# A second order for the same 2445 operations: a two-layer attention and token-MLP kernel whose schedule is a stored list

## The chip, the cores and the metric

The kernel runs on one core of one Trainium2 chip. The metric is the device time of one execution in microseconds (us). Three timed runs of the kernel before gave 452.30, 452.40 and 452.86 us, a median of 452.4 us. One further execution was recorded by the profiler.

## The reference

The input is one sequence of 2048 tokens with 512 features in bf16. Two kinds of block follow each other, each with a layer norm before it and a residual addition after it, and the pair is done twice with the same weights. In the text, layer 0 and layer 1 are the two repetitions.

```python
x = A_x
x = x + _A_ref(_layernorm(x), A_wqkv, A_wo)
x = x + _B_ref(_layernorm(x), B_w1, B_b1, B_w2, B_b2)
x = x + _A_ref(_layernorm(x), A_wqkv, A_wo)
x = x + _B_ref(_layernorm(x), B_w1, B_b1, B_w2, B_b2)
# _A_ref: 32 heads of 16 features; a token sees itself and the 255 before it
scores = einsum("bhqd,bhkd->bhqk", q, k) * 16 ** -0.5      # masked to the window, softmax
o = einsum("bhqk,bhkd->bhqd", softmax(scores), v);  return o @ wo
# _B_ref: an MLP over the tokens, 2048 -> 1792 -> 2048, after a second layer norm
u = gelu(einsum("bsd,sf->bdf", h, w1) + b1);  return einsum("bdf,fs->bds", u, w2) + b2
```

## The kernel before

**The operations.** The kernel first records 2445 operations in a graph (`Graph.op`, L117), each with what it reads and writes. A list then says in which order they are replayed, and for 199 of them which of two or three engines does the work. Line numbers are those of the kernel before; in the kernel after, everything below the list stands 10 lines higher.

On TensorE (915 operations, 6420 matmuls) there are five families.

- A *score* (`f_sc`, L694) multiplies queries and keys of one group of heads. Four heads run in the four row strips of the array at the same time. A score fills two pairs of PSUM banks. There are 76 scores in each layer.
- A *pv* (`f_pv`, L747) multiplies probabilities by values, with 64 by 32 tiles of the array. It needs the exponentials of several scores and their masks.
- *Projections*: queries and keys (`proj`, L566), values (`vproj`, L623, in 64-column tiles), and the output projection (`wo_block`, L783).
- *u*: the first product of the MLP. Most of it (`u_part`, L842) is done while attention still runs, for the token blocks that are ready; the last token blocks come in `u_last` (L861, matmuls at L868).
- *y*: the second product of the MLP (`y_block`, L887), 16 blocks of 7 operations in each layer. The y of layer 0 runs partly beside the attention of layer 1. The y of layer 1 ends the kernel.

All projections, u pieces and y pieces go through one helper, `mm_group`, so that their matmuls have one line, L519. (L521 is the same work done as two 64-column halves, which is used after a value projection.) An operation of `mm_group` is two matmuls of 512 columns.

Beside TensorE: ScalarE does two exponentials for each score (L709), one for each pair of banks, and the gelu (L883). GpSimd multiplies each probability tile with its masks (L730), and takes the power for the layer norm (L490). VectorE does the statistics and the normalising (L477, L479, L497), the transposed read of the attention output out of PSUM (*od*, L767), the reciprocal (L771), a second transpose (*od2*, L778), and the residual additions (L789, L895).

**Choices of engine.** These operations have an alternative: the copies out of PSUM (*evt* L562, *evq* L577, *evk* L599, *evv* L642, *evu* L853) run on VectorE or ScalarE; the first key tiles (*evka*, L588 or L587) run on VectorE or ScalarE; the spreading of keys with zeros (*kz*) is eight small DMAs on the SyncE queue (L608), or two multiplications on GpSimd or VectorE (L613); the product of the attention output with the reciprocal (*prod*, L773) runs on GpSimd or VectorE.

**What sets the order.** Nothing is scheduled when the kernel is built. `begin_order` (L54) unpacks a stored string, `ORDER`, into pairs of an operation and the number of its alternative:

```python
k, alt = divmod(lo + 256 * hi, 4)
out.append((left.pop(k), alt))
```

`Graph.replay` (L185) goes through that list, puts each operation at the end of its engine's program, and hands out buffers as it goes: eight PSUM banks, six probability tiles, four tiles for w1 and so on. A buffer goes to the operation that comes next in the list, and that operation then waits for the buffer's last users (`_take`, L164). So the list settles three things: the order on each engine, the engine, and which earlier work each buffer waits for. `Graph.emit` (L206) writes the programs and their waits. SyncE issues all DMAs in the order of the list, and a DMA that must wait holds up those behind it.

## Time and profile before

| what | value |
|---|---|
| timed runs | 452.30, 452.40, 452.86 us (median 452.4) |
| span of the profiled execution (first to last instruction) | 447.8 us |
| PE busy | 426.7 us (95%) |
| ACT busy | 316.8 us (71%) |
| DVE busy | 307.4 us (69%) |
| POOL busy | 232.2 us (52%) |
| DMA | 41.21 MB, 92 GB/s in the mean |

The profile gives the span of its execution, 447.8 us, and no time of its own beside it. The span is 4.6 us under the median of the timed runs, since these also hold what lies before the first and after the last instruction.

PE stands for TensorE, PEld for its weight loads, DVE for VectorE, ACT for ScalarE, POOL for GpSimd, and SPq for the queue of SyncE. A matmul counts as busy from its start to its modelled end (379 ns for 512 columns), although the next may start 216 ns after it. A PE that is busy throughout is therefore not always a full PE, and distances between starts tell more than busy time.

### The profile page before, as it was taken

The numbers are of one execution on the slowest core, as the hardware profiler recorded it, in microseconds if no ns is written. First come the engines' busy times: TensorE is split into PE (matmuls) and PEld (weight loads), VectorE is DVE, ScalarE is ACT, GpSimd is POOL, SyncE is SP. The second block draws the span as 40 slices with busy tenths as digits, with TensorE's granted clock in tenths as the row PEclk, the third lists the DMA queues.
The fourth block names the chain that finished last, engine by engine and source line by source line (L and its number), as shares of the span: only waits on it lengthen the run. The fifth ranks groups of instructions, "written<-read, shape, count | busy, mean of one in ns | idle before, by whom it ended". The sixth has DMA issues, their size and how long they took to land.

```text
span 447.8 us, 14720 instructions
## 1 busy us (share of the span) xinstructions
PE 426.7 (95%) x6420; PEld 200.4 (45%) x6420; DVE 307.4 (69%) x558; ACT 316.8 (71%) x362; POOL 232.2 (52%) x350
## 2 busy tenths in 40 slices
PE   7988997999989999999999999999899999999997
PEld 6644443334433444444644444444343444444443
DVE  7999789788895478555876767888765577430233
ACT  4999999999898931704898999999999880430000
POOL 5587989866776531010556687768775651000000
PEclk9999999999998999999999999999999999999999
DMA  8240604101153358522132240241223237654435
GB/s 240 68 120 16 132 3 107 15 7 22 25 150 91 73 161 228 144 58 70 26 38 72 57 95 20 55 115 42 51 52 88 74 107 212 174 154 119 119 94 189
DMA packets 95136, 41.21 MB, mean 92 GB/s; under 512 B 33632, under 2 KB 95072, under 8 KB 95072
## 3 DMA queue, kind: packets, MB, share of 16 engines
q1 hardware_dynamic: 95072, 40.27, 35.1%
q8 instruction: 51, 0.84, 0.8%
q14 instruction: 13, 0.11, 0.1%
HBM read 33.56 MB, written 2.10 MB: 80 GB/s over the span
## 4 chain that ended last, share of the span: by engine, by line
PE 65%; ACT 23%; POOL 5%; DVE 4%; DMA 2%; SPq 1%; issue 1%; POOLq 0%
PE PS L519 39%; ACT pt L709 23%; PE PS L868 7%; PE PS L694 7%; PE PS L747 6%; POOL pt L730 4%; PE PS L631 3%; PE PS L521 2%; SPq L608 1%; PE PS L399 1%; DMA w1b<-in_B_w_dram 1%; DVE xh_sb L497 1%; DMA kbd<-stg 1%; DVE rl L767 1%; DVE ul L773 1%
## 5 line engine op out<-in xcount | busy, mean ns | idle before, releaser
L709 ACT ACTIVATE pt<-PS 128x1024 bf16<-128x1024 f32 (+1 forms) x304 | 280.8, 1041 | 19.8 <-PE PS L694 19.2
L730 POOL TENSOR_TENSOR pt<-pt,ldm 128x256 int32<-128x256 int32 (+2 forms) x270 | 176.7, 679 | 74.7 <-ACT pt L709 73.9
L519 PE MATMUL PS<-xh_sb,w1b 128*128 128x512 bf16 x270 | 68.0, 386 | 1.8 <-DVE xh_sb L497 0.8
L694 PE MATMUL PS<-qT,kbd 32*128 32x256 bf16 (+4 forms) x1488 | 60.6, 252 | 6.9 <-ACT pt L709 4.3
L519 PE MATMUL PS<-uT,w2b 128*128 128x512 bf16 x268 | 66.2, 380 | 0.0
L519 PE MATMUL PS<-xhT,wqkv 128*128 128x512 bf16 (+1 forms) x254 | 58.6, 354 | 2.5 <-ACT pt L709 1.0
L490 POOL TENSOR_TENSOR rstd<-agg,mhalf 128x2 f32<-128x2 f32 (+1 forms) x33 | 22.6, 688 | 67.8 <-DVE agg L479 67.7
L767 DVE STREAM_TRANSPOSE rl<-PS 128x1024 f32<-128x1024 f32 x32 | 39.9, 1247 | 22.3 <-PE PS L747 22.0
L895 DVE SCALAR_TENSOR_TENSOR x_sb<-PS,b2col,x_sb 128x512 bf16<-128x512 f32 x32 | 23.6, 742 | 45.0 <-PE PS L519 44.9
L694 PEld LDWEIGHTS PS<-qT,kbd 32*128 32x128 bf16 x1488 | 21.9, 92 | 61.3 <-ACT pt L709 46.1
L883 ACT ACTIVATE uT<-rl,b1col 128x512 bf16<-128x512 f32 x28 | 18.7, 714 | 42.1 <-DVE rl L879 41.7
L747 PE MATMUL PS<-pt,vb 64*32 64x320 bf16 (+4 forms) x2976 | 44.9, 253 | 3.3 <-POOL pt L730 2.0
L477 DVE BATCH_NORM_STATS2 stats<-x_sb 128x6 f32<-128x512 bf16 x64 | 42.9, 678 | 1.4 <-DMA x_sb<-in_A_x_dram 0.7
L519 PE MATMUL PS<-uT,pt 128*128 128x512 bf16 x166 | 40.7, 379 | 0.0
L747 PEld LDWEIGHTS PS<-pt,vb 64*32 64x32 bf16 x2976 | 29.0, 89 | 22.1 <-POOL pt L730 12.6
L868 PE MATMUL PS<-xh_sb,w1b 128*128 128x512 bf16 x168 | 38.6, 379 | 0.2 <-DMA w1b<-in_B_w_dram 0.2
L519 PEld LDWEIGHTS PS<-xh_sb,w1b 128*128 128x128 bf16 x270 | 23.2, 99 | 34.6 <-issue 8.3
L519 PEld LDWEIGHTS PS<-uT,w2b 128*128 128x128 bf16 x268 | 24.5, 98 | 30.3 <-issue 3.2
L631 PE MATMUL PS<-wqkv,xhT 128*64 128x256 bf16 x512 | 35.9, 276 | 1.1 <-ACT pt L709 0.9
L519 PEld LDWEIGHTS PS<-xhT,wqkv 128*128 128x128 bf16 x254 | 21.2, 98 | 26.3 <-issue 4.3
L497 DVE TENSOR_SCALAR xh_sb<-x_sb,agg,rstd 128x512 bf16<-128x512 bf16 x64 | 29.3, 492 | 4.3 <-POOL rstd L490 4.1
L519 PE MATMUL PS<-wo_sb,oT 128*128 128x512 bf16 x122 | 30.6, 380 | 0.6 <-ACT pt L709 0.6
(66 smaller groups left out, 353.2 us busy)
## 6 DMA issues: line engine op xcount, KB each, us to landing
w1b<-in_B_w_dram SPq DMA_DIRECT2D x112, 128.0 KB, 2.8
w2b<-in_B_w_dram SPq DMA_DIRECT2D x70, 128.0 KB, 2.4
pt<-in_B_w_dram SPq DMA_DIRECT2D x42, 128.0 KB, 2.8
out_dram<-x_sb SPq DMA_DIRECT2D x16, 128.0 KB, 1.9
x_sb<-in_A_x_dram SPq DMA_DIRECT2D x3, 512.0 KB, 7.6
kbd<-stg SPq DMA_DIRECT2D x88, 16.0 KB, 1.9
wqkv<-in_A_wqkv_dram SPq DMA_DIRECT2D x4, 256.0 KB, 4.3
wqkv<-in_A_wqkv_dram SPq DMA_DIRECT2D x1, 512.0 KB, 7.0
```

Source lines behind the costliest of these rows:

```text
L477: op("vector:stat", lambda e: e.bn_stats(st[:, 0:6], x_sb[:, t, :]), reads=[f"x{t}"], writes=[("st", i)], cost=dve_cost(512), after=late_s ...
L490: op("gpsimd:rstd", lambda e: e.tensor_tensor(rstd[:, t0:t1, 0], agg[:, t0:t1, 1], mhalf[:, 0:1].to_broadcast([P, t1 - t0]), op=ALU.pow), ...
L497: op("vector:xh", lambda e: e.tensor_scalar(xh_sb[:, t, :], x_sb[:, t, :], agg[:, t, 0:1], rstd[:, t, :], op0=ALU.subtract, op1=ALU.mult), ...
L519: return e.matmul(o, lhsT=w, rhs=x, start=start, stop=stop, skip_group_check=True)
L631: last = e.matmul(bank(ft)[64 * j:64 * j + 64, sc * 256:(sc + 1) * 256], lhsT=xhT[:, tx.slot, c, tok:tok + 64], rhs=wqkv[:, c, 1024:1536]. ...
L694: last = e.matmul(bank(tt[r // 2], r % 2)[:, base + c0 * 64:base + (c0 + n) * 64], lhsT=kbd[32 * r:32 * r + 32, tk.slot, o, jj].rearrange( ...
L709: op("scalar:exp", lambda e, ts=ts, tp=tp, i=i, cols=cols: e.activation(probs(tp)[:, i, 0:cols, :], pair(ts)[:, :, 0:cols].rearrange("p r ...
L730: return e.tensor_tensor(v, v, m, op=ALU.mult)
L747: last = e.matmul(bank(t, h)[32 * r:32 * r + 32, i + q0 * 64:i + (q0 + n) * 64], lhsT=vb[64 * h:64 * h + 64, tk.slot, jj, 4 * o + r, :], r ...
L767: op("vector:od", lambda e, t=tod, tr=tr: e.transpose(rl[:, tr.slot:tr.slot + 2].rearrange("p a b -> p (a b)"), pair(t)), reads=[(tod, i) ...
L868: last = e.matmul(bank(tu, tt), lhsT=v()[:, sc - b0, k0 + tt * P:k0 + (tt + 1) * P], rhs=xh_sb[:, sc, :], start=(sc == b0), stop=(sc == NT ...
L895: op("vector:resy", lambda e: e.scalar_tensor_tensor(x_sb[:, t, :], bank(ft), b2col[:, t:t + 1], x_sb[:, t, :], op0=ALU.add, op1=ALU.add), ...
```

## The change

Only the stored list is replaced. The computation, the sizes, the buffers and the 2445 operations are the same.

```diff
@@ -13,42 +13,32 @@
 ORDER = (
-    'c-qZYJ&5bd6&~5MH}gP&d7!{tP(Z~zP(TC)ROo>o=z#(%6i}hUg$WL*P~pOb3Kb40;KBhHE*wzd!i5SKE?l^9z=aDJE?hX^!o?O2Y~f-',
...
-    'cI+e3L@e4F@kU-y*E#Om5eue-MHQ4AiU_zwVEIC*8S=4>(AaL2tSD4&-+(GKtH=K;SCD};TI|Ym$v@`qvAXq'
+    'c-qZYEvV~S7G7!hc`q~M!hVnkxsZWe$UsCy9%LXQ19^~v3`9h9AR-J$R8&MnRD>a-qM`#85fv2`6%}Eq=s+GsR8&+{R8&+{R8$;MQBiTk5f!u2)1JS3?'
...
+    '6v%IE{{b$XL=O'
 )
```

Unpacked, the two lists differ in the following.

- *Position.* 86 of the 2445 operations keep their place in the list.
- *Engine.* 48 of the 199 choices differ. The number of operations goes from 543 to 555 on VectorE, from 360 to 357 on ScalarE, from 338 to 333 on GpSimd and from 289 to 285 on SyncE (a kz on SyncE, eight DMAs, counted as one). TensorE keeps its 915.
- *prod* goes from 18 on GpSimd and 14 on VectorE to 15 and 17. *kz* goes from 11 on SyncE, 8 on GpSimd and 5 on VectorE to 7, 7 and 10.
- *TensorE.* The scores follow each other in the same sequence. What stands between two scores differs. The array changes between its four layouts (whole, 64-column halves, row strips, 64 by 32 tiles) 350 times, 346 before. Before the first score stand the same six operations.
- *Between the layers*, from the last score of layer 0 to the first of layer 1, stand 47 y operations, 52 before. The other five now stand between scores of layer 1.
- *SyncE.* The first ten loads are as before. The load of x for tokens 1536 to 2047 now stands ahead of the first four transposing DMAs; before, it stood behind them. Weight loads for w1 and w2 are spread differently throughout.
- *The start on ScalarE and VectorE.* The filling of one constant value tile moves from GpSimd to ScalarE, ahead of its first copy; of the first two key tiles one was spread on VectorE and one on ScalarE, and now ScalarE does both, while VectorE takes the first query copies.

## The prediction

> **What bounds the kernel now.** I read the page first: the shares of the engines, and the slices.

> ```profile
> span 447.8 us, 14720 instructions
> PE 426.7 (95%) x6420; PEld 200.4 (45%) x6420; DVE 307.4 (69%) x558; ACT 316.8 (71%) x362; POOL 232.2 (52%) x350
> PE   7988997999989999999999999999899999999997
> ACT  4999999999898931704898999999999880430000
> ```

> TensorE is nearly always busy, ScalarE only in two long stretches: the attention of either layer. So I cut the span at the first and last score of each layer and asked for the busy time in these five stretches (columns: stretch, its length, then each engine's busy time).

> ```profile
> 0.00:8.90 8.90, 5.93 (x56) 5.26 (x56) 5.61 (x17) 2.83 (x5) 5.41 (x15) 1.00 0.76 206
> 8.90:157.10 148.20, 136.02 (x2796) 65.18 (x2796) 120.71 (x226) 139.74 (x156) 110.96 (x162) 0.99 0.29 68
> 157.10:209.80 52.70, 52.68 (x355) 24.20 (x355) 35.43 (x66) 17.28 (x24) 6.81 (x11) 1.00 0.50 140
> 209.80:362.70 152.90, 150.02 (x2737) 68.60 (x2736) 113.18 (x199) 141.82 (x158) 103.80 (x155) 1.00 0.27 60
> 362.70:447.80 85.10, 82.02 (x479) 37.20 (x478) 32.51 (x53) 15.14 (x22) 5.26 (x9) 1.00 0.52 149
> ```

> In layer 0 (8.9 to 157.1) ScalarE is busy 139.7 of 148.2 us and TensorE 136.0: neither is full. In layer 1 TensorE has 150.0 of 152.9. Between the layers TensorE has no gap, and at the end only the last 3 us, in which the output leaves. A new order of the same work can win only where TensorE waits, so I looked at the timeline of TensorE in the worst slice.

> ```profile
> 127.31 0.81 PE L519 MATMUL PS<-wo_sb,oT 128*128 128x512 bf16 x3
> 128.06 0.40 PE L694 MATMUL PS<-qT,kbd 32*128 32x256 bf16 x8
> 128.39 0.60 PE L519 MATMUL PS<-wo_sb,oT 128*128 128x512 bf16 x2
> ...
> 131.47 0.40 PE L694 MATMUL PS<-qT,kbd 32*128 32x128 bf16 x12 [0.59 <-ACT pt L709]
> 132.59 0.41 PE L694 MATMUL PS<-qT,kbd 32*128 32x320 bf16 x8 [0.72 <-DVE rl L767]
> 133.35 1.02 PE L519 MATMUL PS<-xh_sb,w1b 128*128 128x512 bf16 x4 [0.35 <-DVE agg L479]
> 135.14 0.61 PE L694 MATMUL PS<-qT,kbd 32*128 32x64 bf16 x12 [0.77 <-ACT pt L709]
> 135.68 3.27 PE L519 MATMUL PS<-xh_sb,w1b 128*128 128x512 bf16 x8
> ```

> The reader sees two things. Between 131.5 and 135.1 two scores follow each other with nothing between them and little after them, and TensorE waits four times. Then eight matmuls take 3.27 us. At the usual pace they need 1.73 (the chain has 208 of them in 44.91 us, 0.216 each): the granted clock was down. The windows around it:

> ```profile
> 130.00:135.00 5.00, 2.65 (x72) 1.01 (x64) 4.71 (x13) 5.00 (x7) 3.10 (x6) 1.00 0.23 50
> 135.00:140.00 5.00, 4.86 (x32) 1.63 (x32) 1.58 (x3) 3.50 (x5) 5.00 (x9) 0.66 0.25 63
> ```

> In layer 1 the gaps are short waits of pv for masks on GpSimd, such as this one:

> ```profile
> 295.67 0.88 PE L747 MATMUL PS<-pt,vb 64*32 64x64 bf16 x56
> 296.81 0.66 PE L747 MATMUL PS<-pt,vb 64*32 64x64 bf16 x40 [0.27 <-POOL pt L730]
> ```

> **How the change is priced.** The unit is the slot, from one score to the next. TensorE's side is the sum of what the list puts there: 0.432 us for an operation of two 512-column matmuls, 0.23 for a score, 0.47 or 0.70 for a pv, and 0.10 for each change of layout (from the rows above: 127.31 to 128.06 is three matmuls, 0.65, and one change). ScalarE's side is two exponentials, 0.904 each from start to start in the trace, and any copy between them, 0.48. A score waits for the exponential that frees its banks, so a slot lasts about as long as the longer side. Summed for the order before, this gives 145.4 us for layer 0 (measured 148.2) and 151.9 for layer 1 (measured 152.9). The rest, 2.8 and 1.0, are waits that slots do not hold. For the order after I make the same sum and judge the rest.

> **Start, -0.2.** The first score waited 0.66 us on TensorE for VectorE's key tile. That tile now goes to ScalarE, which finishes the first two tiles (two instructions of 476 ns each) before its first exponential. Score earlier, exponential hardly: the gain is at most 0.66, and the second tile can cost up to 0.4. The constant filled on ScalarE first (950 ns on GpSimd) lies in its 3.85 us wait for the first transpose.

> **Layer 0, -1.3.** The slot sum is 145.9, 0.5 more: three more changes of layout, one more u piece, one more ScalarE operation. The rest of 2.8 came from three places: slots around 72 us with a bare score (0.66), the stretch at 130 us with its low clock (1.5), and three output projections that waited 0.6 at 43.7 us. After, the three slots at 72 us hold two matmul operations each; the stretch at 130 us has four u pieces behind its bare score, two before; the projections are two, in a slot with 0.5 us to spare. I leave 1.0 of the 2.8, as one bare score remains. Bounds: -2.3 (nothing left) to +0.5 (all of it back).

> On the clock, the rows say that it fell after 5 us in which TensorE was busy 2.65 and never waited a full microsecond at once. [...]

> **Between the layers, -1.8.** Five y operations of 0.432 leave this stretch, -2.16, where TensorE has no gap that could swallow it. In exchange the first y now stands 1.6 us behind the u that it needs by way of an addition (688 ns) and a gelu (714): at least 1.4 us, and 2.4 in the tightest case before, so it waits 0 to 0.8; I take 0.4. Bounds -2.2 to -1.0.

> **Layer 1, +1.6.** The slot sum is 154.3, 2.4 more: 2.2 are the five y, the rest a change of layout more and less even slots. Five slots before were 0.34 to 0.47 longer than their sum: two pv stood together and the second waited for its mask. In three of these the pv are now one slot apart. They were 1.26 us over, and I count 0.8 as gained. A score whose banks are freed by the exponential just before it occurs 9 times, 8 before; TensorE bounds here, so that costs nothing unless its slot is ScalarE's (0.7 then). Bounds +1.1 (all 1.26 gained) to +3.1 (none, and 0.7 lost).

> SyncE spreads keys 7 times instead of 11. Each time held its queue for some 5.14 us, so four weight loads and transposes get past sooner. The tightest one moves to GpSimd (two of 733 ns) with 5.9 us between its projection and its score: the copy (673), the two instructions and two queued masks of 740 need 3.6, so it is hidden; with five masks ahead it would not be.

> **The end, -0.3.** The same operations stand here. The one DMA wait of before, 0.33 at 389 us, should go: with 0.5 us a DMA on the queue and 2.8 us to landing, I estimate that every load of w1 lands 0.5 us or more ahead of its use, where some had nothing. u pieces now run without y between them, which could leave a gelu late: up to +0.8.

> **Engines at no price.** VectorE gets 12 operations more: 3 products (762), 5 spreads of keys (two of 511 each), the others copies against copies. It is busy 69%, and their cover is its idle time; if that is gone, see the second rival. GpSimd gets 3 products (1077) and one spread less. [...] Eight masks beside such a product took 900 ns in the mean, 170 others 730: by these rows four more products in layer 0 cost GpSimd 0.7 us and save it 4.3, so the sum stays.

> **The sum.** -0.2 -1.3 -1.8 +1.6 -0.3 = **-2.0 us**: a span of 445.8 for 447.8. The median of the timed runs stands 4.6 above the span, which I carry over: **450.4 us**.

> **The rivals.**
> - *No change, 451.5 to 453.3.* The clock falls once more in layer 0 and the masks are as late as before: +1.5 and +0.8 take the gain back, 452.7. For it: a bare score and a thin pv slot still stand together at 130 us, and the masks have only 3.5 to 3.7 us from score to pv in three places. Against: the four u pieces.
> - *Slower: VectorE is late in layer 0, 453.3 to 456.* Between the 16th and the 40th score its work rises by my count of operations, at the distances of their starts, from 34.0 to 39.4 us, of some 46 us. It reads the pv out of PSUM (L767, 1247 ns), and late reads hold up scores: the wait of 0.72 above. If all 5.4 us land on the path the time is 452.4 - 2.0 + 5.4 = 455.8; it is slower than before from 2.9 us on. Against: 46 us hold 39, and from 8.9 to 39.6 us VectorE was busy 29.9 of 30.7, where the slots were only 0.2 us over their sum.
> - *Faster still, 447.6 to 448.9.* Nothing beyond the slots remains: all lower bounds, -0.66 -2.3 -2.2 +1.1 -0.4 = -4.5, give 447.9, less 0.3 for the spread of the runs.

> **How the numbers follow.** A difference under 0.2% (0.9 us) can't be told from none. The likeliest case (448.9 to 451.5) has a chance of 0.38, the faster one 0.14, no change 0.18, slower 0.30. So faster 0.52, same 0.18, slower 0.30. The range is 447.6 to 455.8: it takes in the bounds of the sum and most of the slow rival; the likeliest case alone is 448.9 to 451.5.

> **What would show it.** Right: the stretch from first to last score of layer 0 falls from 148.2 to about 147, the clock row has no dip near 130 us, the stretch between the layers is near 51 us, layer 1 near 154.5. Wrong: waits of scores for L767 grow from the 3.7 us of before (weight loads and matmuls together), a pv waits for L730 oftener, a dip of the clock stands elsewhere, or the end is longer than 85 us.

## The result, and the profile after

Five runs of the kernel after gave 446.34 to 448.23 us, median **447.2 us**, beside five of before with a median of 452.4 (452.0 to 452.86). The ratio is 0.9897, with a 95% interval of 0.9868 to 0.9927. The forecast was 450.4, with a range of 447.6 to 455.8: faster as said, but by 5.2 us instead of 2.0, and just under the range.

The page of the kernel after: the span, the shares of the engines, and two rows of the 40 slices.

```profile
span 446.5 us, 14658 instructions
PE 426.3 (95%) x6396; PEld 200.9 (45%) x6396; DVE 315.6 (71%) x572; ACT 318.1 (71%) x362; POOL 228.6 (51%) x344
PE   7998997899989999999999999999999999999997
ACT  6999999899998942506899899999999880430000
```

The span is only 1.3 us shorter than the 447.8 of the profile before, while the medians stand 5.2 apart. That gap is what the experiments had to explain. Here are the same five stretches as in the prediction, cut at the first and last score of either layer (columns: stretch, length, busy time of PE, PEld, DVE, ACT, POOL, then clock, DMA share, GB/s).

```profile
0.00:8.92 8.92, 6.44 (x60) 5.79 (x61) 4.81 (x18) 4.74 (x6) 4.44 (x14) 1.00 0.76 212
8.92:157.17 148.25, 136.00 (x2798) 65.27 (x2799) 125.64 (x234) 140.64 (x159) 105.92 (x156) 0.99 0.29 68
157.17:207.21 50.04, 50.04 (x347) 22.81 (x348) 33.04 (x62) 16.74 (x23) 6.93 (x11) 1.00 0.46 130
207.21:361.23 154.02, 151.78 (x2731) 70.01 (x2730) 119.98 (x209) 141.25 (x157) 106.01 (x156) 1.00 0.26 64
361.23:446.50 85.27, 81.99 (x479) 37.00 (x478) 32.14 (x53) 14.74 (x21) 5.32 (x9) 1.00 0.51 146
```

Against before the five differ by 0.0, +0.1, -2.7, +1.1 and +0.2 us. The stretch between the layers gave more than forecast, layer 1 cost less, and layer 0, where I expected 1.3, gave nothing in this profile. The timeline of TensorE at the place with the low clock shows why (line numbers are 10 lower than before: L684 is a score, L509 the helper, L757 the read of pv by VectorE).

```profile
130.22 0.40 PE L684 MATMUL PS<-qT,kbd 32*128 32x192 bf16 x8
130.55 0.65 PE L737 MATMUL PS<-pt,vb 64*32 64x64 bf16 x40
131.74 0.40 PE L684 MATMUL PS<-qT,kbd 32*128 32x128 bf16 x12 [0.55 <-ACT pt L699]
133.03 0.40 PE L684 MATMUL PS<-qT,kbd 32*128 32x320 bf16 x8 [0.89 <-DVE rl L757]
133.62 3.53 PE L509 MATMUL PS<-xh_sb,w1b 128*128 128x512 bf16 x8 [0.19 <-DVE xh_sb L487]
```

Two scores still follow each other with a pv before them and nothing between. The four u pieces come after the second one, and their eight matmuls take 3.53 us instead of 1.73: the clock fell here as it did before.

### The profile page after: what moved, and what is told of

Read it like the earlier page. It is cut to its first block, busy times and chain, and to the rows that moved or that the text cites. A ratio compares the mean times of both kernels' runs of the same rounds, so it can differ in the third digit from the quotient of the medians.

```text
span 446.5 us, 14658 instructions
## 1 busy us (share of the span) xinstructions
PE 426.3 (95%) x6396; PEld 200.9 (45%) x6396; DVE 315.6 (71%) x572; ACT 318.1 (71%) x362; POOL 228.6 (51%) x344
## 4 chain that ended last, share of the span: by engine, by line
PE 75%; ACT 11%; DVE 9%; POOL 3%; issue 1%; POOLq 0%
PE PS L509 47%; ACT pt L699 11%; PE PS L858 8%; PE PS L684 7%; PE PS L737 6%; PE PS L621 4%; POOL pt L720 2%; PE PS L511 2%; DVE kbd L603 1%; DVE xh_sb L487 1%; DVE oT L768 1%; PE PS L389 1%; DVE rl L757 1%; DVE x_sb L779 1%; DVE stats L467 1%
## 5 line engine op out<-in xcount | busy, mean ns | idle before, releaser
L509 PE MATMUL PS<-xh_sb,w1b 128*128 128x512 bf16 x272 | 68.8, 388 | 1.4 <-DVE vb L632 0.7
L684 PE MATMUL PS<-qT,kbd 32*128 32x256 bf16 (+4 forms) x1488 | 60.2, 251 | 7.6 <-ACT pt L699 4.3
L509 PE MATMUL PS<-uT,w2b 128*128 128x512 bf16 x274 | 67.3, 380 | 0.0
L509 PE MATMUL PS<-xhT,wqkv 128*128 128x512 bf16 (+1 forms) x266 | 61.3, 357 | 2.6 <-ACT pt L699 0.7
L757 DVE STREAM_TRANSPOSE rl<-PS 128x1024 f32<-128x1024 f32 x32 | 39.9, 1246 | 22.2 <-PE PS L737 22.0
L480 POOL TENSOR_TENSOR rstd<-agg,mhalf 128x2 f32<-128x2 f32 (+1 forms) x33 | 23.8, 721 | 56.3 <-DVE agg L469 54.0
L684 PEld LDWEIGHTS PS<-qT,kbd 32*128 32x128 bf16 x1488 | 21.9, 92 | 62.9 <-ACT pt L699 41.3
L509 PE MATMUL PS<-uT,pt 128*128 128x512 bf16 x168 | 40.7, 379 | 0.1
L509 PEld LDWEIGHTS PS<-uT,w2b 128*128 128x128 bf16 x274 | 25.2, 98 | 31.1 <-issue 3.3
L509 PEld LDWEIGHTS PS<-xh_sb,w1b 128*128 128x128 bf16 x272 | 23.7, 99 | 33.5 <-issue 7.5
L621 PE MATMUL PS<-wqkv,xhT 128*64 128x256 bf16 x512 | 34.4, 276 | 0.8 <-ACT pt L699 0.7
L509 PEld LDWEIGHTS PS<-xhT,wqkv 128*128 128x128 bf16 x266 | 22.0, 98 | 27.7 <-issue 6.8
L487 DVE TENSOR_SCALAR xh_sb<-x_sb,agg,rstd 128x512 bf16<-128x512 bf16 x64 | 29.9, 485 | 3.5 <-POOL rstd L480 3.4
L509 PE MATMUL PS<-wo_sb,oT 128*128 128x512 bf16 x124 | 31.0, 380 | 1.0 <-DVE kbd L603 0.6
```

Source lines behind the costliest of these rows:

```text
L480: op("gpsimd:rstd", lambda e: e.tensor_tensor(rstd[:, t0:t1, 0], agg[:, t0:t1, 1], mhalf[:, 0:1].to_broadcast([P, t1 - t0]), op=ALU.pow), ...
L487: op("vector:xh", lambda e: e.tensor_scalar(xh_sb[:, t, :], x_sb[:, t, :], agg[:, t, 0:1], rstd[:, t, :], op0=ALU.subtract, op1=ALU.mult), ...
L509: return e.matmul(o, lhsT=w, rhs=x, start=start, stop=stop, skip_group_check=True)
L621: last = e.matmul(bank(ft)[64 * j:64 * j + 64, sc * 256:(sc + 1) * 256], lhsT=xhT[:, tx.slot, c, tok:tok + 64], rhs=wqkv[:, c, 1024:1536]. ...
L684: last = e.matmul(bank(tt[r // 2], r % 2)[:, base + c0 * 64:base + (c0 + n) * 64], lhsT=kbd[32 * r:32 * r + 32, tk.slot, o, jj].rearrange( ...
L757: op("vector:od", lambda e, t=tod, tr=tr: e.transpose(rl[:, tr.slot:tr.slot + 2].rearrange("p a b -> p (a b)"), pair(t)), reads=[(tod, i) ...
```

## The clock goes by a grid of 3.41 us

The record of the granted clock explains this and the gap between span and median. In the traces of this case the record of the full clock begins between 4.4 and 7.7 us, at 5.37 in before and at 7.40 in after. Counted from that moment, every later stretch at half clock ahead of the last matmul (19 of them in 12 traces, the experiments' included) begins at a whole multiple of 3.413 us, within 0.02 of a multiple, and lasts 3.41 us or twice that. In before it begins at 135.07 us, 129.71 or 38 such steps later, in after at 133.70, 126.29 or 37 steps later. So in these traces the clock changes window by window, and where the windows lie differs from execution to execution. Here are windows of that grid: two of before, three of after, two of the experiment dense_130b (PE's busy time stands after the length, the clock third from the end).

```profile
131.66:135.07 3.41, 1.64 (x24) 0.46 (x12) 3.15 (x8) 3.41 (x5) 2.09 (x4) 1.00 0.17 32
135.07:138.49 3.42, 3.35 (x19) 1.20 (x20) 0.85 (x3) 2.76 (x4) 3.42 (x6) 0.50 0.12 20
```

```profile
130.30:133.71 3.41, 1.79 (x69) 0.82 (x69) 3.41 (x11) 3.20 (x5) 2.27 (x4) 1.00 0.17 29
133.71:137.12 3.41, 3.41 (x14) 0.97 (x16) 2.34 (x5) 2.56 (x3) 3.03 (x6) 0.50 0.14 36
75.69:79.10 3.41, 1.85 (x25) 0.62 (x26) 3.41 (x7) 2.96 (x5) 3.41 (x6) 1.00 0.00 0
```

```profile
130.01:133.42 3.41, 2.27 (x72) 1.00 (x64) 3.41 (x10) 3.20 (x5) 2.26 (x5) 1.00 0.07 10
133.42:136.84 3.42, 3.01 (x30) 1.00 (x30) 2.55 (x5) 3.36 (x6) 3.04 (x5) 1.00 0.49 137
```

After a window with PE busy 48% or 52% the next one runs at half clock; after 54% and 66% it does not. In all the traces the limit lies in a band: half clocks that begin follow windows of 56% at most, and all windows under 47% were followed by one; between the two both occur (the 52% above was followed by one, a window of y_back from 212.06 us, busy 1.80 of 3.41 or 53%, was not), so PE's busy share as the profile has it does not decide alone. No wait in the windows of before and after reaches a full microsecond (the longest is 0.89): here windows half full were enough.

A thin place of some 4 us is therefore hit or missed by chance. Before had two of them, at 72 and 131 us, after has one and a milder one at 75. Sliding the grid over the traces, with a limit of 54%, I estimate that before is hit 0.7 times an execution at either place, and after 0.35 and 0.17 times; with 56% it would be 2.1 times in all for before and 0.7 for after. One window at half clock lowers the mean granted clock of an execution by 3.41 x 0.5 / 447.5 = 0.004, so that each timed execution tells how many it had:

| kernel | executions | half-clock windows, mean | median span with none | with one | with two | time less span |
|---|---|---|---|---|---|---|
| before (three comparisons, and the two runs of its copies below) | 87 | 1.84 | 447.3 | 448.2 | 449.1 | 2.11 |
| after (two comparisons) | 11 | 0.45 | 444.7 | 446.5 | - | 1.74 |

Over the 87 executions of before each such window costs 1.16 us (a straight line through span and count); in the eleven of after, too few to be exact, the one window goes with 1.8. The profile before, with one window at 447.8, was quicker than most of its kind. So the change takes 1.7 to 2.6 us at the same number of windows, 1.4 windows of 1.16 us, that is 1.6, and 0.4 outside the span: 3.7 to 4.6 us, against 5.2 in the first comparison and 3.6 in the second.

## The experiments

Each kernel was compared with before on the same chip. The lists are text, so the edits are shown on the unpacked list: `fu` is an operation of u (two matmuls), `evu` the copy of a finished u out of PSUM, `fy` a y, `resy` the addition behind it, `fv` and `evv` a value projection and its copy, `sc` a score, `exp` and `mask` its followers, `w1_` a load of w1, and numbers are operations. Where the expectations of dense_130 and dense_130b say u piece, they mean two `fu`, and by gelu the copy `evu`.

### Half of the list at a time

The kernel before unchanged, after once more, and the two halves crossed at the last score of layer 0.

```diff
 # new0_old1                          # old0_new1
-after, all of it                     -before, all of it
+after, up to sc 862                  +before, up to sc 862
+the rest as in before                +the rest as in after
```

> The kernel before, unchanged, against itself. The timed gain of the new order is 5.2 us, but the profiled spans differ by 1.3 us alone (447.8 and 446.5), so 3.9 us have to be found. Theory 'transfers': the spans of the timed runs are about 450 to 451, longer than the profiled 447.8, because some loads come later there. Theory 'outside': the spans are near 447.8 and 4.6 us lie outside the span, against 1.7 for the new order. Theory 'clock': the granted clock is 0.996 in every run, with a span of 447.8, and the new order's runs split in those with 0.996 and those with 1.0.

> The changed kernel once more, on the same chip as the mixed orders. All theories: 446.3 to 448.2 us, spans 444.6 to 446.5, the runs with a granted clock of 0.996 some 1.5 us longer than those with 1.0. If the clock does not split the runs, the spread has another cause.

> The new list up to the last score of layer 0, the old list for all that is left. The stage sum and the two profiles say that layer 0 itself is not shorter (148.2 us in both), so by 'stages' this is within 1 us of the kernel before, 451.4 to 452.6 us. By 'transfers', with the tight loads of the old list all behind the middle, it is also as before, 452. By 'clock' it is shorter by up to 1.7 us in the runs in which the clock does not fall.

> The old list up to the last score of layer 0, the new one for the rest. By 'stages' it takes the 2.6 us between the layers and gives back 1.1 in layer 1: some 450.9 us. By 'transfers' it takes nearly the whole gain, 447 to 448.5 us. By 'clock' it stays near 450.5 with 0.996 in every run.

| kernel | median us | ratio to before (95%) | half-clock windows, mean | last score L0 to first of L1 | layer 1 |
|---|---|---|---|---|---|
| before_again | 451.3 (12 runs) | 0.9995 (0.9974 to 1.0017) | in the 87 above | 53.3 | 153.5 |
| after_again | 448.0 (6) | 0.9910 (0.9875 to 0.9944) | 0.5 | 50.0 | 154.0 |
| new0_old1 | 448.9 (12) | 0.9943 (0.9920 to 0.9965) | 0.33 | 53.3 | 153.3 |
| old0_new1 | 448.8 (12) | 0.9948 (0.9920 to 0.9976) | 1.67 | 50.4 | 154.3 |

Before stood at 451.6 here. The halves take 2.7 and 2.8 us, and they do not do it in the same way. The half with the new layer 0 keeps the old time between the layers and has few half-clock windows; the half with the new rest has the short stretch between the layers and nearly as many half-clock windows as before. That is the split of the table above. At the same number of windows old0_new1 is 1.6 us under before (445.7, 446.6 and 447.5 us with none, one and two), and new0_old1 between 0.5 under and 0.4 over it (446.8 and 448.6 with none and one). The theories 'stages' and 'clock' had 450.5 to 450.9 for old0_new1 and missed it by 2 us; 'stages' had 451.4 or more for new0_old1. The profile of new0_old1 fell on a grid that missed the thin places:

```profile
8.38:155.50 147.12, 134.37 (x2795) 64.76 (x2796) 125.94 (x235) 140.48 (x159) 105.95 (x156) 1.00 0.29 70
```

That is 147.1 us for the new layer 0 without a half clock, where after, with one window, has 148.25. The old layer 0 was never profiled without one. With one window each, the new one takes 148.1 to 148.4 us (after, after_again, pv_back, y_back) and the old one 147.7 to 148.2 (before, before_again, old0_new1): at the same clock the new order gains nothing in layer 0. Layer 1 takes 154.0 to 154.4 us in seven traces with the new rest (153.9 in y_back) and 152.5 to 153.5 in four with the old.

Between the layers the profile of before, 52.7 us, was the quick one. In before_again, before_rewrapped and new0_old1 this stretch takes 53.3 us, and in each TensorE waits 0.6 or 0.7 us there for a load of w1, as here in before_again:

```profile
169.35 3.20 PE L519 MATMUL PS<-xh_sb,w1b 128*128 128x512 bf16 x14 [0.70 <-DMA w1b<-in_B_w_dram]
```

No trace with the new rest, in order and engines, has that wait. So 'transfers' was right in a small part: the stretch is 2.7 us shorter in the first pair of profiles and 3.3 in the others. The time outside the span is 1.7 in both halves, 2.1 in before_again; 'outside', which wanted 4.6, is refuted.

### The five y, and the three pairs of pv

Two terms of my sum, undone one at a time in the kernel after.

```diff
 # y_back: in front of the first score of layer 1
 fy1321 fy1322
+fy1323 resy1324 fy1307 resy1308 fy1293 fy1294 fy1295
 sc1193
-fy1323 ... resy1324
 ...
 sc1198
-fy1307 resy1308 fy1293 fy1294 fy1295
```

> The kernel after with five y operations (0.432 us each on TensorE, 2.16 together) and two sums that end in them moved from the first two slots of layer 1 back in front of the first score of layer 1. Theory 'moved time' (my sum: 2.16 leave one stretch and 2.2 enter the other): last score of layer 0 to first score of layer 1 grows from 50.0 to 52.2, first to last score of layer 1 falls from 154.0 to 151.8 or 152, and the median is that of after within 0.4 us; the gain of the change then lies in other places. Rival 'filler': in layer 1 the five filled slots that ScalarE or a mask sets, so that layer 1 falls by 1.2 us or less and the median is 1 us or more above that of after.

449.4 us (447.85 to 450.58, 12 runs), ratio 0.9969 (0.9950 to 0.9988). With no half-clock window the span is 447.1, which is the 447.3 of before within the spread, and 2.4 above after. The stretch between the layers grows to 52.19, just the 2.16 of five y. But layer 1 does not fall: 153.89 us against 154.03. The rival "filler" holds. This is TensorE in the second slot of layer 1, in y_back and then in after_again:

```profile
211.97 0.60 PE L508 MATMUL PS<-uT,pt 128*128 128x512 bf16 x2
214.08 0.40 PE L683 MATMUL PS<-qT,kbd 32*128 32x320 bf16 x8 [1.51 <-ACT pt L698]
```

```profile
210.25 2.33 PE L509 MATMUL PS<-uT,pt 128*128 128x512 bf16 x10
212.51 0.40 PE L684 MATMUL PS<-qT,kbd 32*128 32x320 bf16 x8
```

Without the four y the third score waits 1.51 us for an exponential; with them it waits for nothing. ScalarE in y_back shows why that wait is so long:

```profile
209.64 1.94 ACT L698 ACTIVATE pt<-PS 128x1024 bf16<-128x1024 f32 x2 [2.52 <-PE PS L683]
212.09 1.94 ACT L698 ACTIVATE pt<-PS 128x1024 bf16<-128x1024 f32 x2 [0.51 <-PE PS L683]
```

The scores start at 209.19, 211.63 and 214.08, the second and third just after the two exponentials of the score before have ended (211.58 and 214.03). Score and exponentials take turns, 0.5 and 1.94 us, so the slot lasted 2.45 with only two matmuls more in it (the row at 211.97). With the y it lasts 2.59 (209.92 to 212.51 in after_again). The y stand in time that TensorE would for the most part have spent waiting.

```diff
 # pv_back: slots 42, 47 and 62 of layer 1, one of them
 sc1719 ... pv1703
+pv1714
 sc1723
-pv1714
```

> The kernel after with the second pv of three pairs in layer 1 (42nd, 47th and 62nd score) put back directly behind the first, as before. Theory 'late masks' (my 0.8): waits of pv for a mask grow by 0.8 to 1.3 us over the 0.8 of after, first to last score of layer 1 grows from 154.0 to 154.8 or more, the median rises by 0.5 to 1.3 us. Rival 'no wait': the masks are there, and the median is that of after within 0.3 us.

447.0 us (446.31 to 447.97, 6 runs), ratio 0.9910 (0.9880 to 0.9940). The wait of pv for masks returns, as the lists of waits show for after and then for pv_back:

```profile
PE PS L737 <- POOL pt L720: 0.8, 3, 0.4
```

```profile
PE PS L736 <- POOL pt L719: 2.0, 4, 0.9
```

Layer 1 becomes 154.43, 0.4 longer, for 1.2 us more of waiting: most of it is made up at the scores behind. The ratio is that of after_again, 0.9910. Without a half clock the span is 445.2 (444.6 to 445.5, five runs) where after has 444.7 (444.5 to 446.1, six). The term was 0.4 in layer 1, not 0.8, and too small to be told apart in the time.

### Order against choice of engine

```diff
 # new_order_old_engines              # old_order_new_engines
-(operation, engine) of after         -(operation, engine) of before
+(operation of after,                 +(operation of before,
+ engine of before)                   + engine of after)
```

> The order of all operations from the kernel after, the engine of each operation from the kernel before. Theory 'order' (my steps priced the choice of engines at nothing): within 0.5 us of the kernel after, which took 448.0 beside 451.6, so a ratio to before near 0.992. Rival 'engines': the products and spreads that changed engine carry the gain, and this kernel is within 1 us of before, ratio 0.998 or more.

> The order of before with the engines of after. Theory 'order': within 1 us of before, ratio 0.998 to 1.002, granted clock mostly 0.992 as in the runs of before. Rival 'engines': 2 us or more faster, ratio 0.996 or less.

479.6 us, ratio 1.0637 (1.0597 to 1.0677), and 472.5 us, ratio 1.0483 (1.0460 to 1.0507): both far slower than either kernel, which neither theory expected. The lists of waits show part of where it goes, here two of the longest of each (new_order_old_engines first).

```profile
PE PS L508 <- DMA w2b<-in_B_w_dram: 8.6, 3, 4.9
PE PS L683 <- DVE qT L566: 4.4, 4, 3.3
```

```profile
PE PS L684 <- POOL kbd L603: 3.7, 1, 3.7
PE PS L509 <- DVE qT L567: 2.2, 1, 2.2
```

With the old engines SyncE has 11 spreads of keys again, where the new order has room for 7. One of the four more, in new_order_old_engines on SyncE's queue:

```profile
249.58 5.14 SPq L597 DMA_DIRECT2D kbd<-stg  x8
254.76 3.66 SPq L804 DMA_DIRECT2D w2b<-in_B_w_dram  x7
```

The seven loads of w2 stand behind it, and TensorE waits 1.4 and 2.3 us for w2 at 258 and 261 us. The longest such wait, 4.9, is at 307 us, behind another of the four, which holds the queue from 299.7 to 304.8. With the new engines in the old order a score at 305 us waits 3.7 us for a spread that now is GpSimd's and stands there behind five masks. These waits are a part of the 21 to 28 us; the rest was not taken apart. "Engines at no price" was right only for engines together with the order written for them.

### Filling and emptying the thin places

```diff
 # dense_130: after, layer 0
 sc658 ... fu545 fu546 evu547
-fu537 fu534
 sc752 ...
-fu535 evu536 fu538 evu539
 ...
-w1_969 w1_971 w1_968          (behind sc658, sc756 and sc782)
 sc791 exp792
+fu534 fu535 fu537 fu538
 sc797 ... exp793
+evu536 evu539
 ...
+w1_969 w1_971 w1_968          (ahead of the spread kz709 on SyncE)
```

> The kernel after with two u pieces (four operations of 0.432 us on TensorE) taken from scores 55 and 56 of layer 0 and put behind the bare score at 131.7 us, their two gelus into ScalarE's wait that follows, and one w1 tile loaded 20 us later for it. Theory 'clock by density' (the half clock at 133.7 us follows from the thin slots at 130 us): no half clock between 125 and 145 us in the profile, a mean granted clock of 1.0 in most runs, first to last score of layer 0 near 147.0 instead of 148.3, and a median 0.5 to 1.5 us under that of after (about half of its runs had no half clock anyway). Rival 'clock elsewhere': TensorE is as often at half clock as in after, about one time in two runs, at another place, and the time is that of after within 0.3 us. [...]

One thing more differs from after: the copy evu539 went from ScalarE to VectorE. 455.2 us (451.87 to 456.17, 6 runs), ratio 1.0083 (1.0053 to 1.0113): slower than before, a miss by 8 us. SyncE's queue and one score in dense_130, and then the same queue in after_again:

```profile
119.39 16.69 SPq L792 DMA_DIRECT2D w1b<-in_B_w_dram  x12
136.12 6.11 SPq L597 DMA_DIRECT2D kbd<-stg  x8
```

```profile
143.59 0.61 PE L683 MATMUL PS<-qT,kbd 32*128 32x256 bf16 x8 [2.97 <-DMA kbd<-stg]
```

```profile
119.49 7.04 SPq L793 DMA_DIRECT2D w1b<-in_B_w_dram  x12
126.57 6.03 SPq L598 DMA_DIRECT2D kbd<-stg  x8
```

The loads that I had moved wait for the buffer that the moved u pieces free late, and the spread of keys behind them on the same queue began 9.6 us later. A score then waited 2.97 us; the window around this wait was 39% busy, and two windows at half clock follow (from 142.7 us). Layer 0 took 155.4, 7.0 more than in after_again; the slot of the wait and the two behind it are 5.6 us longer than there. The kernel was mended by letting one u piece stay, with its copy on ScalarE, and putting the loads behind the spread:

```diff
 # dense_130b: after, layer 0
 sc791 exp792
+fu537 fu538
 sc797 ... exp793
+evu539
 ... kz709 w1_970
+w1_969 w1_971 w1_968
```

> The kernel dense_130 with its fault taken out: one u piece (two operations of TensorE) instead of two goes behind the bare score at 131.7 us, its gelu stays on ScalarE, and the w1 tile that waits for it is loaded behind the spread of keys instead of ahead of it on SyncE's queue. Theory 'queue' (dense_130 was slow because the spread of keys began 9.6 us late behind those loads): no wait of a score for a spread at 140 us, and a median within 1 us of after. Theory 'clock by density' on top: no half clock between 125 and 145 us, first to last score of layer 0 near 147.2, median 0.5 us or more under that of after. Rival to the second: the half clock comes all the same, first to last score near 148.3.

447.3 us (447.01 to 447.77, 6 runs), ratio 0.9921 (0.9894 to 0.9949). The wait for the spread is gone, and the 8 us with it: by the trace of dense_130 most of them were that wait and the half clock behind it. Three things were taken back at once, so the rest, some 1.4 us of layer 0, is not divided among them. None of the six executions had a half-clock window; of the 41 executions of kernels with the layer 0 of after (after, y_back, pv_back, new0_old1) 15 had one. Layer 0 falls to 147.56. If the chance were 15 in 41 for each, six in a row without one would come about in 7 of 100 cases: this speaks for the density, together with the 66% of the window above, and does not prove it. The time is no better than that of after or pv_back, since the piece itself costs there: its slot grows from 1.28 to 1.88 us, and the slots that it left do not shrink. The span is 445.55 where after without a half clock has 444.7. No version faster than after was found.

```diff
 # bare_72: after, layer 0
 sc387 ...
-fv463 fv464 evv465
 sc393 ...
 sc398 exp399 exp400 mask402
+fv463 fv464 evv465
```

> The kernel after with one v projection (two operations, 0.432 us each, on TensorE) moved from the 34th score of layer 0 to the 36th, so that this score at 72 us stands bare, as it did before. Theory 'clock by density': the half clock comes oftener, mean granted clocks of 0.992 among the runs as in before, and the median is 1 to 2 us above that of after. Rival 'slots only': the bare score costs the 0.3 to 0.7 us of its own wait and the granted clock is as in after.

447.2 us (445.95 to 448.8, 6 runs), ratio 0.9922 (0.9898 to 0.9945): not slower. The mean number of half-clock windows was 0.83, against 0.37 in the 41 executions. In the profile a new one stands at 75.8, after a window with PE busy 1.65 of 3.41 us (48%). The direction is that of the clock theory, but with six runs the count is inconclusive, and the 1 to 2 us that I had expected did not show; the intervals, 1 us and more to either side, do not rule out the lower end.

### Outside the span

```diff
 # before_rewrapped
-ORDER of before in lines of its own lengths
+the same ORDER in lines of 118 characters, as in after
```

> The kernel before, instruction for instruction, with its list written in lines of the length that after uses. It bears on the 0.35 us by which the time stands further above the span before (2.1) than after (1.7). Theory 'program': the 2.1 belong to the instructions, and stay; time as before within 0.3 us. Rival 'file': the time outside the span hangs on something other than the instructions, and falls to 1.7.

450.8 us (12 runs), ratio 1.0006 (0.9983 to 1.0028). The time less the span stays at 2.06 to 2.18, so it belongs to the program. Every kernel with another list than that of before, the slow ones too, had medians of 1.7 to 1.8 (1.7 to 2.0 in single executions). What part of the list does it stays open. This profile shows the other thin place of before, hit (windows of 5 us, clock third from the end):

```profile
70.00:75.00 5.00, 3.31 (x135) 1.86 (x136) 4.65 (x8) 5.00 (x6) 4.44 (x7) 1.00 0.69 178
75.00:80.00 5.00, 4.08 (x30) 1.40 (x24) 4.24 (x7) 4.04 (x5) 5.00 (x8) 0.50 0.63 73
```

## Why the prediction was right or wrong

The sign was right, and two of the reasons given for it hold: the y that left the stretch between the layers, and, in the mean over executions, the clock. The forecast missed by 3.2 us: 2.9 of it is the carry-over and 0.3 the span (445.8 forecast, 445.5 in the run with the median time). That the span came so near is partly luck. That run had no half-clock window and the profile it is set against had one (1.16 us), and single terms are off by up to 0.9 in both directions.

- **From span to median, "4.6 above the span, which I carry over": wrong.** The time stands 2.1 above the span of its own execution in before and 1.7 in after; only these lie before the first and after the last instruction, and not the 4.6 that the section on time and profile explains in this way. Of the other 2.5, 1.0 is that the profiled execution had one half-clock window where before has 1.84 in the mean, and 0.4 that it was quicker than the median of those with one (448.2). The last 1.1 is that the five runs of before in the first comparison were slower (452.4) than those of later ones (450.5 to 451.6); their clock is not on record, so this part stays open. I took a difference between executions for a constant of the program.
- **Layer 0, -1.3: in the clock alone, and as a matter of chance.** At the same number of half-clock windows the layer did not get shorter (148.25 us after, 148.20 before). "Four u pieces behind its bare score" did not keep the clock up: they come after the window that decides. What the list changed is the chance of being hit, from 1.84 to 0.45 windows an execution, some 1.6 us in the mean, where the sum held one window missed for certain. The half clock came after windows 48% and 52% busy, in which no wait was longer than 0.89 us, and did not come after the 66% of dense_130b: this fits denser slots that keep the clock up.
- **Between the layers, -1.8: -2.7.** The five y are 2.16, as y_back measured. Counting again, the stretch also lost one operation of u (22 instead of 23), 0.43, which I had added to the slots of layer 0 and not taken from here: 2.59 in all. The wait of the first y behind its gelu, for which I had taken 0.4, did not come: PE is busy 50.04 of 50.04 us. Against the further traces with the old rest the gain is 3.3, since these have the wait for a load of w1 that the profile of before was spared.
- **Layer 1, +1.6: +1.1, by other terms.** It is 0.6 to 1.5 against the further traces. "2.2 are the five y" was wrong: in the first two slots they cost hardly more than waiting did, 153.89 without them and 154.03 with them. What grew is the part from the 17th to the 37th score, 40.4 to 41.5, where TensorE has five y more and two query operations fewer than before, while 37th to 57th fell from 40.1 to 39.4, 0.6 of it by the pv that pv_back put back (40.0 there). The slot model erred where it took the longer of two sides: y_back shows that a score freed by the exponentials just before it makes its slot 2.45 us long, not 1.81, and the first slots of layer 1 are such slots. How much of the 0.5 under the forecast this explains is not shown.
- **Start, -0.2: 0.0,** within its bounds. The wait of 0.7 for the key tile is gone, and the first score came at the same time all the same.
- **End, -0.3: +0.2.** The wait for the load of w1 went, but the last matmul came no more than 0.04 us sooner after the last score. No matmul waited for a late gelu. Over all traces the end takes 85.1 to 85.4 us with the old order there and 84.8 to 85.8 with the new, so neither sign is shown.
- **The slower rival did not come.** VectorE had 125.6 us to do in layer 0 instead of 120.7; the waits of scores for its read of pv grew from 3.7 to 4.9 us over the kernel, weight loads and matmuls together, but in layer 0 they fell from 3.3 to 2.7.
- **"Engines at no price"** held for this pair of kernels. The two crossed kernels show how narrow that is. The product beside which eight masks took 900 ns is one on VectorE; in the profile after, nine masks of 128x256 beside such a product took 834 ns in the mean and the 193 others 736. What makes them longer is not shown.
- **"Faster still, 447.6 to 448.9"** is the case next to what came, 447.2, but not by its mechanism: the slots did not reach all their lower bounds. The half clock of "no change" did come, in the profile and in 5 of 11 executions, and the time fell all the same.
- **The signs** were to be read from one profile, and it misleads: the dip near 130 us stayed, the waits for the read of pv grew, the end is over 85 us, and yet the kernel is faster by more than forecast.

## What to carry to other kernels

Before a span is compared with a median, read the granted clock of both: this kernel, whose TensorE is half idle for some 4 us at a place, lost about 1.2 us there in part of its executions and not in others, and one profile did not tell the mean. Filler for such a place is to be tried ahead of the second score, before the window ends: in after it stood behind that score and the half clock came in 5 of 11 executions, while dense_130b had it ahead and none came in six. Work moved into a slot that waits for another engine was nearly free (0.14 us for 2.16), and a load that must wait for a buffer belongs behind, not ahead of, whatever its queue must deliver next (in dense_130 the spread of keys behind such loads began 9.6 us later).
